# Linear attention and MLP, two layers: loads reordered, key projections split, output buffers shared, new instruction lists

## The chip, the cores and the metric

One core of a Trainium2 chip. The metric is the device time in microseconds of one execution, as the median of several runs. Engines: PE (TensorE, matrix products), DVE (VectorE), ACT (ScalarE), POOL (GpSimd), and SP (SyncE), which here only issues DMA transfers. PE writes into PSUM banks; the others read these.

## The reference

Two identical layers, each an attention block and an MLP block, on x of 2048 rows by 512 columns in bf16:

```python
def _A_ref(x, wqkv, wo):          # H = 32 heads of 16
    q, k, v = qkv[0], qkv[1], qkv[2]
    phi = lambda t: jnp.where(t > 0, t + 1, jnp.exp(t)) + 1e-6
    pq, pk = phi(q), phi(k)
    kv = jnp.einsum("bhsd,bhse->bhde", pk, v)
    z = jnp.einsum("bhsd->bhd", pk)
    num = jnp.einsum("bhqd,bhde->bhqe", pq, kv)
    den = jnp.einsum("bhqd,bhd->bhq", pq, z)[..., None] + 1e-6
...
def _B_ref(x, w1, b1, w2, b2):    # F = 1792
    y = _layernorm(x, axis=-1)
    h = _gelu(jnp.einsum("bsd,df->bsf", y, w1) + b1)
    return jnp.einsum("bsf,fd->bsd", h, w2) + b2
...
x = x + _A_ref(_layernorm(x, axis=-1), A_wqkv, A_wo)
x = x + _B_ref(_layernorm(x, axis=-1), B_w1, B_b1, B_w2, B_b2)
```

The last two lines stand there twice, with the same weights.

## The kernel before

The 2048 rows are 16 tiles of 128 rows, in four chunks of four tiles. In the first attention block the chunks are worked in the order 3, 0, 1, 2, so tiles 12 to 15 come first. All weights stay in SBUF. Names carry the layer, then the tile or chunk: `K0_12` is the key projection of tile 12 in layer 0.

**The steps of an attention block.** A tile of x is normalized (`stats`, `aggr` on DVE, `veps` and `pow` for the reciprocal root, then `cen` and `ysc`, or `norm`). Its normalized rows are transposed, by PE (`PT...`, then a copy `tc...` on ACT) or by a DMA transpose that SP issues (`TA...` before attention, `TB...` before the MLP, `TP...` for queries). `K` multiplies by the key weights: four products of 512 columns, one for each 128 rows of the weights. `Q` does so with the query weights. phi is an exponential and a relu on ACT (`exp`, `relu`), a clipped sum (`min`) and a sum (`phi`) on DVE or POOL; phi(K) goes into one of eight buffers `pk`. `G` accumulates y-transposed times phi(K) over all tiles, so that the value projection is applied once at the end (`KV`), masked to heads (`kvm`) and multiplied by wo (`M`). `Z` and `zs` sum phi(K); `D` gives the denominators, and `WO` the block's output, added to x by `RA`. In layer 1, G is summed by chunk on DVE (`ga`, `gt`) before KV.

**The steps of the MLP.** `W1` (line L1133) is the up-projection: four products for each of 14 blocks of hidden columns. For chunk 0 it is done in halves of two tiles, 256 columns at a time (names end in `_0` and `_1`); for the others on all four tiles, 512 columns. ACT applies gelu. `W2` (L1171) is the down-projection of a tile in two half-sums of seven products (`_0` and `_7`), and `RB` adds it to x. In the last MLP `RB` writes to one of two buffers `outb`, which `OD` stores from SP's queue. The very last tile, 15, is done in two column halves of 256 (`h0`, `h1`; L1158, L1163, L1165), each with its own store.

**What sets the order.** Each engine runs one fixed list of names, written out in `CONF["ORDER"]`. A planner (`Scheduler`) walks the lists with estimated durations and hands out buffers and PSUM banks in the order of that plan; `assign_waits` turns every dependence into a semaphore wait. An engine takes its list strictly in order, so a late operand holds all behind it. DMA issues are entries of the SP, ACT or POOL list.

**The start.** SP's list begins `x0 x1 wk0 x2 wq xc0 xc1 xc2`: the rows of tile 12, of tile 13, the first half of the key weights, the rows of tiles 14 and 15 (`x2`, 256 KB), the query weights (`wq`, 512 KB), then chunks 0, 1 and 2. ACT issues the second half of the key weights (`wk1`). While nothing can be multiplied PE runs dummy products of constants (`warm`: eight of 512 columns and `N_WARM2` of 128; `idle0_0` and `idle0_1`: `N_IDLE` of 128 after each of the first two transposes).

Of the kernel before, what the change touches and what calls it, by code (L numbers as in the profile page):

```python
# [6 lines left out]
BF16 = mybir.dt.bfloat16  # L7
# [20 lines left out]
DMA_LAT = 800.0  # L28

# [81 lines left out]
class Scheduler:  # L111
# [12 lines left out]
    def run(self):  # L124
# [13 lines left out]
        bus = 0.0  # L138
        for _ in g.ops:
            best = None  # L140
            for e in ENGINES:
                if len(self.order[e]) == len(queue[e]):
                    continue
                o = queue[e][len(self.order[e])]
                if o.missing:
                    continue
                at = max(o.ready, free[e])
                if o.table is not None and o.table != table:
                    at = max(o.ready, free[e] + TABLE_LOAD)
# [17 lines left out]
            dur = o.dur  # L167

            if o.fast and pool_busy > at:
                dur += pool_busy - at - 60.0  # L170
            if o.fast:
                dve_busy = at + dur
            if e == "pool" and o.sem is None and o.dur > 300.0:
                dur += max(0.0, min(dve_busy - at, 400.0))
                pool_busy = at + dur
# [92 lines left out]
def assign_waits(graph, order, sems, dma_sems):  # L268
# [10 lines left out]
    while len(done) < total:  # L279
        moved = False  # L280
        for e in ENGINES:
# [43 lines left out]
    N_WARM2=1, N_IDLE=[4, 3], XQ='sp', WKQ='sp act', WK1=1,  # L325
    LAND={'x0': 3210, 'x1': 3930, 'wk1': 5300, 'wk0': 6430, 'x2': 6950, 'wq': 8450, 'xc0': 9730, 'xc1': 11020, 'xc2': 12240},
# [5 lines left out]
            "warm PTA0_12 idle0_0 PTA0_13 idle0_1 K0_12 K0_13 PTA0_14 Q0_3_0 Q0_3_2 PTA0_15 K0_14 K0_15 G0_12_0 "  # L332
            "Q0_3_1 G0_13_0 Q0_3_3 G0_14_0 PTA0_1 K0_0 G0_15_0 K0_1 Z0_3 G0_0_0 K0_3 K0_2 Q0_0_2 G0_1_0 Q0_0_0 "
            "K0_8 K0_4 G0_2_0 G0_3_0 K0_6 Q0_0_3 G0_4_0 K0_7 K0_5 K0_10 K0_11 Z0_0 K0_9 Z0_1 Q0_1_2 Q0_1_0 Q0_1_3 "
            "Q0_0_1 Z0_2 G0_5_0 G0_6_0 D0_0_0 D0_0_3 G0_7_0 Q0_1_1 G0_8_0 D0_0_1 G0_9_0 D0_0_2 G0_10_0 G0_11_0 "
            "G0_11_2 D0_1_0 G0_11_1 Q0_2_0 G0_11_3 KV0_0 D0_1_1 KV0_1 KV0_2 D0_1_2 ZR0 KV0_3 Q0_2_1 M0_0 M0_2 M0_1 "
            "M0_3 Q0_2_2 WO0_0_0 WO0_0_1 WO0_0_2 WO0_0_3 D0_1_3 WO0_1_0 WO0_2_0 WO0_3_0 Q0_2_3 WO0_4_0 WO0_6_0 "
            "WO0_7_0 PTB0_0 WO0_5_0 W10_0_5_0 W10_0_1_0 W10_0_7_0 W10_0_9_0 W10_0_6_0 W10_0_3_0 W10_0_2_0 "
            "W10_0_4_0 W10_0_12_0 W10_0_13_0 W10_0_0_0 W10_0_10_0 W10_0_11_0 W20_0_0 W10_0_8_0 W20_1_0 W20_1_7 "
            "W20_0_7 W10_0_8_1 W10_0_1_1 W10_0_7_1 W10_0_9_1 W10_0_5_1 W10_0_12_1 W10_0_0_1 W10_0_3_1 W10_0_11_1 "  # L340
            "W10_0_13_1 W10_1_3_0 W10_1_4_0 W10_1_13_0 W10_1_11_0 WO0_8_0 W10_1_0_0 WO0_9_0 W10_1_2_0 W10_0_6_1 "
            "W10_0_2_1 W10_0_4_1 W10_1_8_0 W10_1_12_0 W10_1_7_0 W10_1_5_0 W10_1_10_0 WO0_11_0 W10_1_6_0 W10_1_1_0 "
            "WO0_10_0 W10_1_9_0 W20_4_0 W20_7_0 W20_7_7 W20_4_7 W20_5_0 WO0_15_0 K1_0 W20_2_0 W20_5_7 W20_6_0 "
            "W20_6_7 K1_1 W10_2_10_0 W10_2_3_0 W10_2_0_0 W10_0_10_1 WO0_14_0 W10_2_13_0 WO0_12_0 W10_2_6_0 "
            "WO0_13_0 W20_2_7 W10_2_11_0 W10_2_5_0 W10_2_8_0 W10_2_7_0 W10_2_1_0 W10_2_4_0 W10_2_2_0 W10_2_9_0 "
            "W10_2_12_0 W20_9_0 W20_8_0 W20_9_7 W20_8_7 W20_3_0 W20_3_7 W20_10_0 W20_11_0 K1_4 K1_2 W10_3_1_0 "
            "W10_3_7_0 W10_3_8_0 W10_3_5_0 W20_10_7 W10_3_0_0 W10_3_3_0 W20_11_7 W10_3_9_0 W10_3_6_0 W10_3_10_0 "
            "W10_3_2_0 K1_3 W10_3_13_0 W10_3_4_0 W10_3_12_0 W10_3_11_0 K1_8 K1_5 G1_0_1 G1_0_3 G1_0_0 K1_6 G1_0_2 "
            "W20_12_0 K1_7 W20_12_7 W20_13_0 W20_13_7 W20_14_0 K1_9 K1_10 G1_1_0 W20_15_0 W20_15_7 W20_14_7 K1_11 "
            "Q1_1_1 Q1_1_0 G1_1_1 G1_1_3 G1_1_2 Q1_0_0 K1_13 K1_12 Q1_1_2 G1_2_1 Q1_0_2 K1_14 K1_15 Q1_0_1 Q1_1_3 "  # L350
            "ZH1 Q1_0_3 Z1_3 G1_2_2 G1_3_1 D1_0_0 ZR1 G1_2_0 D1_0_2 G1_3_2 D1_0_1 G1_3_3 G1_3_0 G1_2_3 Q1_3_0 "
            "KV1_0 KV1_1 Q1_3_1 KV1_2 D1_0_3 Q1_3_2 KV1_3 Q1_2_0 M1_1 M1_0 M1_3 M1_2 Q1_2_1 WO1_0_0 Q1_3_3 WO1_0_1 "
            "WO1_1_0 WO1_0_2 WO1_0_3 WO1_3_0 WO1_2_0 Q1_2_2 WO1_5_0 WO1_4_0 PTB1_1 Q1_2_3 PTB1_0 WO1_6_0 "
            "W11_0_13_0 W11_0_10_0 W11_0_12_0 W11_0_4_0 WO1_7_0 W11_0_0_0 W11_0_5_0 W11_0_7_0 W11_0_1_0 W11_0_3_0 "
            "W11_0_11_0 W11_0_6_0 W11_0_9_0 W11_0_8_1 W11_0_11_1 W11_0_4_1 W11_0_3_1 W11_0_8_0 W11_0_0_1 W11_0_5_1 "
# [12 lines left out]
            "normA0_3 tcA0_1 expk0_0 expq0_3_3 reluq0_3_3 expk0_1 reluk0_1 normA0_8 normA0_6 reluk0_3 expk0_3 "
            "expk0_2 reluq0_0_2 expq0_0_2 normA0_7 expk0_8 normA0_10 expk0_4 reluq0_0_0 normA0_5 reluk0_6 normA0_9 "
            "expq0_0_3 expk0_6 expk0_7 expq0_0_0 expk0_5 reluk0_5 expk0_10 expk0_11 reluk0_11 expk0_9 reluk0_9 "  # L370
            "reluq0_1_2 expq0_1_2 expq0_1_3 expq0_1_0 expq0_0_1 reluq0_0_1 ln0_0_0 ln0_0_3 rec0_0_0 rec0_0_3 "
            "expq0_1_1 ln0_0_1 rec0_0_1 reluq0_1_1 ln0_0_2 rec0_0_2 ln0_1_0 expq0_2_0 rec0_1_0 ln0_1_1 cpz0 "
            "rec0_1_1 cpm0_0 cpm0_1 cpm0_3 ln0_1_2 rec0_1_2 ln0_1_3 rec0_1_3 expq0_2_2 reluq0_2_1 reluq0_2_2 "
            "reluq0_2_3 expq0_2_1 expq0_2_3 b1c tcB0_0 gelu0_0_5_0 gelu0_0_1_0 gelu0_0_9_0 gelu0_0_6_0 gelu0_0_7_0 "
            "gelu0_0_3_0 gelu0_0_4_0 gelu0_0_12_0 gelu0_0_2_0 gelu0_0_0_0 gelu0_0_11_0 gelu0_0_8_0 gelu0_0_10_0 "
            "gelu0_0_13_0 gelu0_0_8_1 gelu0_0_1_1 gelu0_0_9_1 gelu0_0_7_1 gelu0_0_5_1 gelu0_0_12_1 gelu0_0_0_1 "
            "gelu0_0_13_1 gelu0_0_11_1 gelu0_0_3_1 gelu0_1_13_0 gelu0_1_3_0 gelu0_1_0_0 gelu0_1_11_0 gelu0_1_4_0 "
            "gelu0_0_6_1 gelu0_0_2_1 gelu0_1_2_0 gelu0_1_8_0 gelu0_1_12_0 gelu0_1_5_0 gelu0_1_10_0 gelu0_1_6_0 "
            "gelu0_1_7_0 gelu0_1_1_0 gelu0_1_9_0 gelu0_0_4_1 normA1_1 expk1_0 normB0_9 normB0_11 gelu0_2_3_0 "
            "gelu0_0_10_1 gelu0_2_10_0 gelu0_2_13_0 expk1_1 gelu0_2_6_0 gelu0_2_0_0 reluk1_0 gelu0_2_11_0 "  # L380
# [152 lines left out]
def build_kernel(nc, A_x, A_wqkv, A_wo, B_x, B_w1, B_b1, B_w2, B_b2, out, conf=None, report=False):  # L533
# [5 lines left out]
    with ExitStack() as es:  # L539
# [3 lines left out]
        def mksem(name):  # L543
            return Sem(es.enter_context(nc.semaphore(name)), name)

        NT4, NYB, NPK, NER, NGT, NLR, NSTAT, NOUT = 12, 10, 8, 4, 2, 2, 12, 2
        xsb = SB("xsb", [P, ST, D], FP32)
        t4 = SB("t4", [P, NT4, 4 * D], BF16)
        wqkv = SB("wqkv", [P, DT, 3 * D], BF16)
# [818 lines left out]
```

## Time and profile before

| | us |
|---|---|
| median of 3 runs (328.71, 328.74, 331.37) | 328.74 |
| span of the profiled execution | 326.2 |
| PE busy with matmuls | 320.6 |
| DVE busy | 218.7 |
| ACT busy | 197.5 |
| POOL busy | 131.2 |

The span goes from the first to the last instruction of one profiled execution; the runs' time holds what lies around it. The page is read with one warning: a matmul's record is longer than the time by which it holds up the next one, so a busy PE of 98% says that something was always in its pipeline and not that it ran at its best rate. How far apart matmuls start says more. The granted PE clock was 1.000 over the span.

Busy time by stretch (columns: stretch, its length, busy us and number of instructions of PE, weight loads, DVE, ACT and POOL, granted clock, share of DMA, GB/s):

```profile
0.00:20.00 20.00, 17.82 (x102) 8.15 (x103) 14.42 (x46) 16.06 (x29) 9.93 (x27) 1.00 0.51 171
20.00:60.00 40.00, 40.00 (x250) 19.05 (x248) 34.71 (x90) 35.36 (x65) 23.70 (x38) 1.00 0.46 130
160.00:210.00 50.00, 49.71 (x263) 22.95 (x262) 43.59 (x102) 32.11 (x58) 27.18 (x34) 1.00 0.11 22
275.00:327.00 52.00, 48.65 (x240) 23.21 (x237) 9.39 (x16) 17.44 (x28) 1.53 (x1) 1.00 0.14 38
```

### The profile page before, as it was taken

To read this page: it belongs to the slowest core of one execution; us is meant where nothing else is said; L and a number is where in the kernel's file an instruction comes from. 1 tells how busy PE (TensorE), PEld (TensorE's weight loads), DVE (VectorE), ACT (ScalarE), POOL (GpSimd) and SP (SyncE) were. 2 spreads that over 40 slices of the span, in tenths; PEclk is the share of its full clock that TensorE was granted. 3 is DMA by queue.
4 is the path that set the end of the run, shared out by engine and by line. 5 is a ranking of instruction groups with operands and counts; after the bars stand their busy time and mean duration, and the time that the engine had idled before them with its cause. 6 is when DMAs were issued, how large, how long until landed. Compare 5 with 4: busy or idle time off the path is not lost.

```text
span 326.2 us, 4796 instructions
## 1 busy us (share of the span) xinstructions
PE 320.6 (98%) x1724; PEld 158.2 (48%) x1724; DVE 218.7 (67%) x506; ACT 197.5 (61%) x338; POOL 131.2 (40%) x224
## 2 busy tenths in 40 slices
PE   7999999999999999999999999999999999999996
PEld 3444545656544444444444444458644444444453
DVE  4998689989866662535468899999988663300132
ACT  5998889744753387357963395969923553645200
POOL 3465637673238106134139525645811275100000
PEclk9999999999999999999999999999999999999999
DMA  7424662524012400312110200111153233300011
GB/s 239 163 51 92 173 223 62 181 49 81 21 31 48 97 1 2 74 22 55 27 32 19 47 17 0 28 39 36 32 92 72 48 45 69 81 0 2 32 64 50
DMA packets 47028, 20.39 MB, mean 62 GB/s; under 512 B 41948, under 2 KB 45532, under 8 KB 47004
## 3 DMA queue, kind: packets, MB, share of 16 engines
q1 hardware_dynamic: 45676, 15.09, 20.4%
q0 software_dynamic: 1056, 4.72, 4.5%
q10 hardware_dynamic: 272, 0.26, 0.3%
q8 instruction: 14, 0.23, 0.3%
q14 instruction: 10, 0.08, 0.1%
HBM read 8.00 MB, written 2.10 MB: 31 GB/s over the span
## 4 chain that ended last, share of the span: by engine, by line
PE 91%; DVE 4%; DMA 2%; ACT 1%; SPq 1%; issue 1%; ACTq 0%
PE ps L1133 29%; PE ps L1171 26%; PE ps L1101 9%; PE ps L852 9%; PE ps L870 5%; PE ps L953 4%; PE ps L883 3%; PE ps L985 2%; DMA t<-in_A_x_dram 1%; PE ps L1158 1%; DMA t<-yb 1%; DVE t L839 1%; PE ps L1008 1%; PE ps L1077 1%; PE ps L797 1%
## 5 line engine op out<-in xcount | busy, mean ns | idle before, releaser
L1139 ACT ACTIVATE gT<-ps,b1c 128x512 bf16<-128x512 f32 (+1 forms) x140 | 76.9, 601 | 61.2 <-PE ps L1133 60.8
L1133 PE MATMUL ps<-t,w 128*128 128x512 bf16 (+1 forms) x560 | 102.2, 336 | 0.5 <-DMA t<-yb 0.3
L1171 PE MATMUL ps<-w,gT 128*128 128x512 bf16 x434 | 97.3, 379 | 0.0
L1133 PEld LDWEIGHTS ps<-t,w 128*128 128x128 bf16 x560 | 54.4, 98 | 44.5 <-DMA t<-yb 0.7
L1171 PEld LDWEIGHTS ps<-w,gT 128*128 128x128 bf16 x434 | 42.4, 98 | 50.4 <-ACT gT L1139 0.3
L822 ACT ACTIVATE eb<-ps 128x512 bf16<-128x512 f32 x56 | 32.1, 606 | 21.3 <-PE ps L852 20.3
L749 POOL TENSOR_TENSOR rstd<-veps,neghalf 128x1 f32<-128x1 f32 x64 | 36.7, 581 | 8.2 <-DVE veps L747 5.5
L1181 DVE TENSOR_TENSOR outb<-ps,xsb 128x512 bf16<-128x512 f32 x15 | 10.3, 689 | 40.3 <-PE ps L1171 32.1
L734 DVE BATCH_NORM_STATS2 stats<-xsb 128x6 f32<-128x512 f32 x48 | 32.0, 681 | 0.2
L1101 PE MATMUL ps<-gtb,t 128*128 128x512 bf16 x128 | 31.8, 379 | 0.1
L852 PE MATMUL ps<-wqkv,t 128*128 128x512 bf16 x128 | 31.1, 379 | 0.0
L769 ACT ACTIVATE yb<-xsb,nmr,rstd 128x512 bf16<-128x512 f32 x21 | 16.8, 811 | 12.6 <-POOL nmr L766 12.5
L833 ACT ACTIVATE rb<-ps 128x512 bf16<-128x512 f32 x38 | 22.3, 611 | 1.6 <-PE ps L852 0.9
L739 POOL TENSOR_SCALAR veps<-mv 128x1 f32<-128x1 f32 x32 | 7.3, 227 | 38.4 <-DVE mv L736 36.6
L774 DVE TENSOR_SCALAR yb<-xsb,mv,rstd 128x512 bf16<-128x512 f32 x27 | 15.0, 572 | 9.0 <-POOL rstd L749 8.9
L835 DVE TENSOR_SCALAR eb<-eb 128x512 bf16<-128x512 bf16 x46 | 13.6, 306 | 10.9 <-ACT eb L822 10.8
L1118 POOL TENSOR_TENSOR xsb<-xsb,b2b 128x512 f32<-128x512 f32 x14 | 17.0, 1218 | 8.1 <-DVE yb L774 6.5
L870 PE MATMUL ps<-wqkv,t 128*128 128x512 bf16 x80 | 20.2, 379 | 0.0
L747 POOL TENSOR_SCALAR veps<-mv 128x1 f32<-128x1 f32 x28 | 8.4, 305 | 28.0 <-DVE mv L736 26.9
L1101 PEld LDWEIGHTS ps<-gtb,t 128*128 128x128 bf16 x128 | 12.3, 98 | 14.9 <-ACT gtb L966 0.7
L852 PEld LDWEIGHTS ps<-wqkv,t 128*128 128x128 bf16 x128 | 12.0, 97 | 14.7 <-ACT t L807 0.9
L1065 POOL TENSOR_TENSOR t<-t,rr 128x512 bf16<-128x512 bf16 x7 | 7.7, 1100 | 24.4 <-DVE rr L1061 14.1
(103 smaller groups left out, 398.7 us busy)
## 6 DMA issues: line engine op xcount, KB each, us to landing
w<-in_B_w_dram POOLq DMA_DIRECT2D x4, 896.0 KB, 5.9
out_dram<-outb SPq DMA_DIRECT2D x15, 128.0 KB, 2.1
t<-in_A_x_dram SPq DMA_DIRECT2D x3, 512.0 KB, 7.3
t<-yb SPq DMA_TRANSPOSE x56, 2.5
wqkv<-in_A_wqkv_dram SPq DMA_DIRECT2D x1, 512.0 KB, 5.7
wo<-in_A_wo_dram POOLq DMA_DIRECT2D x1, 512.0 KB, 6.6
wqkv<-in_A_wqkv_dram POOLq DMA_DIRECT2D x1, 512.0 KB, 4.5
t<-t SPq DMA_TRANSPOSE x20, 2.5
```

Source lines behind the costliest of these rows:

```text
L734: G.op("dve", lambda e: e.bn_stats(stats[:, s.slot, :], src()), 620, reads=src_keys, writes=[k + "s"], tiles=[s, *src_tiles], prio=prio, n ...
L749: G.op("pool", lambda e: e.tensor_tensor(rstd[:, s.slot:s.slot + 1], veps[:, s.slot:s.slot + 1], neghalf[:], op=ALU.pow), 570, reads=[k + ...
L769: G.op("act", lambda e: e.activation(yb[:, y.slot, :], src(), ACT.Identity, bias=nmr[:, s.slot:s.slot + 1], scale=rstd[:, s.slot:s.slot + 1]),
L822: G.op("act", lambda e: e.activation(eb[:, et.slot, :], bank(bt), ACT.Exp, scale=factor()), 478, reads=[src_key, *more], writes=[f"e{tag}" ...
L833: G.op("act", lambda e: e.activation(rb[:, rt.slot, :], bank(bt), ACT.Relu, scale=factor()), 478, reads=[src_key, *more], writes=[f"r{tag} ...
L852: ins = e.matmul(bank(b), lhsT=yTa(yT)[:, dt, k * P:(k + 1) * P], rhs=wqkv[:, dt, D:2 * D], start=(dt == 0), stop=(dt == DT - 1))
L870: ins = e.matmul(bank(b), lhsT=yTa(yT)[:, dt, k * P:(k + 1) * P], rhs=wqkv[:, dt, 0:D], start=(dt == 0), stop=(dt == DT - 1))
L1101: ins = e.matmul(bank(wb), lhsT=yTa(pq)[:, kt, k * P:(k + 1) * P], rhs=gtb[:, kt, :], start=(kt == 0), stop=(kt == DT - 1))
L1118: G.op("pool" if on_pool else "dve", lambda e: e.tensor_tensor(xsb[:, st, :], xsb[:, st, :], b2b[:], op=ALU.add), 1120 if on_pool else 600 ...
L1133: ins = e.matmul(bank(b, n), lhsT=w1[:, dt, ft * P:(ft + 1) * P], rhs=yTa(yT)[:, dt, k0 * P:k1 * P], start=(dt == 0), stop=(dt == DT - 1))
L1139: G.op("act", lambda e, ft=ft, b=b, k0=k0, k1=k1, n=n: e.activation(gT[:, g.slot, ft * 512 + k0 * P:ft * 512 + k1 * P], bank(b, n), ACT.Ge ...
L1171: ins = e.matmul(bank(b), lhsT=gT[:, g.slot, ft * 512 + k * P:ft * 512 + (k + 1) * P], rhs=w2[:, ft, :], start=(ft == 0), stop=(ft == FT - 1))
```

## The change

The computation is the same, but for the order of the four products summed in two key projections. The edits:

1. SP's list begins `x0 x1 wk0 wq x2`: the query weights are issued ahead of the rows of tiles 14 and 15.
2. `K0_12` and `K0_13` are each split into two pairs of products; the pair on `wk1` goes first (`K0_12_0`), the pair on `wk0` second (`K0_12`).
3. The dummies: `N_WARM2` 1 to 4, `N_IDLE` [4, 3] to [8, 1].
4. The buffers `outb` are gone; the last block writes to the eight phi(K) buffers. There are 12 buffers of normalized rows for 10.
5. The last tile is split into 384 and 128 columns for 256 and 256.
6. All five lists are written anew, after changes in the planner's durations (which act on its plan alone, and so on the buffers handed out).

```diff
+TAIL = 384
...
-    N_WARM2=1, N_IDLE=[4, 3], XQ='sp', WKQ='sp act', WK1=1,
+    N_WARM2=4, N_IDLE=[8, 1], XQ='sp', WKQ='sp act', WK1=1, K_SPLIT=2, K_HALVES=(1, 0),
...
         "pe":
-            "warm PTA0_12 idle0_0 PTA0_13 idle0_1 K0_12 K0_13 PTA0_14 Q0_3_0 Q0_3_2 PTA0_15 K0_14 K0_15 G0_12_0 "
+            "warm PTA0_12 idle0_0 K0_12_0 K0_12 PTA0_13 idle0_1 Q0_3_0 K0_13_0 K0_13 Q0_3_1 PTA0_14 G0_12_0 PTA0_15 "
+            "K0_14 K0_15 Q0_3_3 Q0_3_2 G0_13_0 K0_0 G0_14_0 PTA0_1 G0_15_0 K0_1 G0_0_0 Z0_3 K0_3 K0_2 Q0_0_2 G0_1_0 "
...
-            "W10_0_4_0 W10_0_12_0 W10_0_13_0 W10_0_0_0 W10_0_10_0 W10_0_11_0 W20_0_0 W10_0_8_0 W20_1_0 W20_1_7 "
-            "W20_0_7 W10_0_8_1 W10_0_1_1 W10_0_7_1 W10_0_9_1 W10_0_5_1 W10_0_12_1 W10_0_0_1 W10_0_3_1 W10_0_11_1 "
-            "W10_0_13_1 W10_1_3_0 W10_1_4_0 W10_1_13_0 W10_1_11_0 WO0_8_0 W10_1_0_0 WO0_9_0 W10_1_2_0 W10_0_6_1 "
+            "W10_0_11_0 W10_0_2_0 W10_0_0_0 W10_0_12_0 W10_0_9_0 W10_0_13_0 W20_0_0 W20_1_0 W10_0_0_1 W10_0_2_1 "
+            "W10_0_12_1 W10_0_5_1 W10_0_11_1 W20_0_7 W10_0_4_1 W20_1_7 W10_0_13_1 W10_0_7_1 W10_0_6_1 W10_0_1_1 "
+            "W10_0_3_1 WO0_8_0 W10_0_8_1 W10_0_9_1 W10_0_10_1 W20_2_0 W20_3_0 W20_3_7 W20_2_7 WO0_11_0 W10_1_5_0 "
...
+            "ZR1 D1_0_0 G1_3_0 G1_2_0 D1_0_1 G1_2_3 G1_3_3 G1_3_2 D1_0_2 Q1_3_1 Q1_3_0 KV1_0 D1_0_3 KV1_1 KV1_2 KV1_3 "
...
+            "WO1_5_0 WO1_3_0 PTB1_1 Q1_2_3 PTB1_0 WO1_4_0 WO1_6_0 W11_0_8_0 W11_0_3_0 WO1_7_0 W11_0_10_0 W11_0_7_0 "
+            "W11_0_0_0 W11_0_4_0 W11_0_5_0 W11_0_12_0 W11_0_9_0 W11_0_13_1 W11_0_12_1 W11_0_2_0 W11_0_5_1 W11_0_1_0 "
...
         "dve":
+            "ones statsA0_12 aggrA0_12 vepsA0_12 cenA0_12 negA0_13 yscA0_12 cenA0_13 yscA0_13 mink0_12 statsA0_14 "
+            "statsA0_15 aggrA0_14 aggrA0_15 cenA0_14 phik0_12 cenA0_15 statsA0_0 vepsA0_14 aggrA0_0 statsA0_3 "
...
         "pool":
-            "powA0_9 nmrA0_5 nmrA0_9 vepsA0_11 powA0_11 phik0_6 w2_0 bdm1 wo phiq0_1_2 wv w1_0 phiq0_1_1 pr0_0_2 "
-            "pr0_1_0 pr0_1_1 w1_1 pr0_1_2 pr0_1_3 vepsB0_1 powB0_1 vepsB0_0 powB0_0 w2_1 pz0_2_1 phiq0_2_3 "
+            "nmrA0_7 vepsA0_11 powA0_11 phik0_6 bdm1 w1_0 w1_1 wv wo w2_1 w2_0 phiq0_1_2 phiq0_1_1 pr0_0_2 pr0_1_0 "
...
         "sp":
-            "x0 x1 wk0 x2 wq xc0 xc1 xc2 TA0_0 TA0_3 TA0_2 TA0_8 TA0_4 TA0_6 b1 TA0_7 TA0_10 TA0_5 TA0_11 TA0_9 b2 "
+            "x0 x1 wk0 wq x2 xc0 xc1 xc2 TA0_0 TA0_3 TA0_2 b1 TA0_8 TA0_4 TA0_10 TA0_5 TA0_6 TA0_7 TA0_11 TA0_9 b2 "
...
-            "OD1 TP1_2_1 TB1_12 TB1_14 OD2 TB1_13 TB1_15 OD4 TB1_11 TB1_9 OD5 TB1_8 TB1_10 OD7 OD14 OD6 OD9 OD12 "
+            "TB1_14 TB1_13 TB1_15 TB1_12 TB1_8 TB1_10 TB1_11 OD2 OD6 OD4 TB1_9 OD15_0 OD5 OD14 OD7 OD12 OD10 OD13 OD8 "
+            "OD9 OD11 OD15_1",
...
-        NT4, NYB, NPK, NER, NGT, NLR, NSTAT, NOUT = 12, 10, 8, 4, 2, 2, 12, 2
+        NT4, NYB, NPK, NER, NGT, NLR, NSTAT = 12, 12, 8, 4, 2, 2, 12
...
+            if L == 0 and c == HC and k < cf["K_SPLIT"]:
+                halves = cf["K_HALVES"]
+                for i, h in enumerate(halves):
+                    def part(e, h=h, i=i):
+                        n = DT // len(halves)
+                        for j in range(n):
+                            ins = e.matmul(bank(b), lhsT=yTa(yT)[:, n * h + j, k * P:(k + 1) * P], rhs=wqkv[:, n * h + j, D:2 * D],
+                                           start=(i == j == 0), stop=(i == len(halves) - 1 and j == n - 1))
+                        return ins
...
-                ot = Tile(OUT, f"out{st}")
+                ot = Tile(PK, f"out{st}")
...
-                    cs = slice(h * D // 2, (h + 1) * D // 2)
+                    cs = slice(0, TAIL) if h == 0 else slice(TAIL, D)
```

## The prediction

> **What bounds the kernel now.** I read the first page for engine shares and the chain, then TensorE's own timeline through the first 12 us, then the chain of waits where TensorE restarts late, and last the two ends: the landing times of the loads and the final stores.
>
> ```profile
> PE 320.6 (98%) x1724; PEld 158.2 (48%) x1724; DVE 218.7 (67%) x506; ACT 197.5 (61%) x338; POOL 131.2 (40%) x224
> ...
> PE 91%; DVE 4%; DMA 2%; ACT 1%; SPq 1%; issue 1%; ACTq 0%
> ```
>
> TensorE is the bound: 98% busy, 91% of the chain. Its matmuls run at one 512-column product per 0.216 us (eight in 1.73 us in the chain), a group of four in 0.865, and the change leaves the number of useful ones alone. So only the places where TensorE stands still can be won. First the start:
>
> ```profile
> 4.57 0.40 PE L797 MATMUL ps<-idp,yb 128*128 128x128 bf16 x4 [0.37 <-DVE yb L715]
> 4.80 0.39 PE L690 MATMUL ps<-const-bfloat16-1.0 128*128 128x128 bf16 x4
> 6.14 0.40 PE L797 MATMUL ps<-idp,yb 128*128 128x128 bf16 x4 [0.94 <-DVE veps L747]
> 6.37 0.33 PE L690 MATMUL ps<-const-bfloat16-1.0 128*128 128x128 bf16 x3
> 6.55 1.89 PE L852 MATMUL ps<-wqkv,t 128*128 128x512 bf16 x8
> ```
>
> The first key projections start at 6.55, behind the second tile's transpose, though the first tile's copy ended at 5.99 and the key weights were there. After 8.4 us I list every place where the next matmul starts over 0.06 us later than the last one's 0.216 us allow: 8.44 (0.17), 11.75 (0.19), 20.29 (0.13), 36.4 (0.14), 78.8 (0.41), 203.3 (0.43), 206.1 (0.19), 210.4 (0.10), 247.05 (0.28), 272.07 (0.42). From 19 us on that is 2.1 us, 2.3 with the small change. The chain shows the large ones:
>
> ```profile
> 78.56 0.25 issue
> 78.81 1.24 PE ps L1133 x5
> ...
> 202.07 1.20 DVE gtb L998 x2
> 203.27 0.05 issue
> 203.32 0.62 PE ps L1008 x8
> ...
> 266.75 1.51 SPq L1183
> 268.31 1.19 SPq L784
> 269.54 2.49 DMA t<-yb
> 272.07 4.49 PE ps L1133 x20
> ```
>
> At 78.8 the first full-width up-projection of chunk 1 waits for a transpose issued at 74.74 that landed at 78.72. At 203.3 KV waits for VectorE's sum of G. At 272.07 it is a transpose held on SP's queue by an output store (L1183, 1.51 us). The ends:
>
> ```profile
> wqkv<-in_A_wqkv_dram SPq DMA_DIRECT2D x1, 512.0 KB, 5.7
> t<-in_A_x_dram SPq DMA_DIRECT2D x1, 256.0 KB, 4.8
> ...
> 323.69 0.43 DVE L1163 TENSOR_TENSOR outb<-ps,xsb 128x256 bf16<-128x256 f32 x1 [0.69 <-PE ps L1158]
> 324.14 0.33 SPq L1165 DMA_DIRECT2D out_dram<-outb  x1
> ```
>
> Query weights: issued 2.69, landed 8.4. Rows of tiles 14 and 15: issued 2.19, landed 7.0. The last store is issued 0.48 after the last matmul ends (323.66) and lands at 325.72.
>
> **The start, part by part.** The loads after wk0 share one stream (wk0 in at 6.24, 256 KB more at 6.95, 512 KB more at 8.42). Swapped, the query weights land at 6.24 + 1.47 = 7.7 and tiles 14/15 at 8.4, 1.4 later; each issue takes 0.42 to 0.47 on SP, so nothing behind them moves. The 3 extra warm dummies (0.056 each) and 4 more in the first idle group lie in TensorE's waits of 0.37 and 0.94; without that cover they cost 0.39, and two fewer in the other group give 0.11 back.
> TensorE anew: first copy in at 5.99, so K12 runs 6.07 to 6.93 (the half on wk1, in by 5.5, goes first; wk0 is in at 6.24, before the third matmul at 6.50). The transpose of tile 13 follows to 7.16, then it waits 0.55 for the query weights: Q0_3_0 7.7 to 8.6, K13 to 9.5, Q0_3_1 to 10.35. VectorE meanwhile gets tile 14 at 8.4: two stats at 0.60, two aggregates, centring 0.27 give 10.25, so the transpose of tile 14 is just in time; phi of tile 12 is next (10.6), G12 10.65 to 11.5, transpose 15 to 11.7, K14 to 12.6, K15 to 13.5 (its copy on ScalarE, by 0.57 a scaled exp or relu and 0.48 a copy, is done at 12.55). Carried on alike, thirteen groups and the transposes are through at 18.9; the row of before has thirteen at 18.89. So 0.5 sooner at the start is paid back as a wait for the query weights: net 0. Bounds: -0.3 if all of it is just in time, +1.3 if VectorE, idle for 6.4 to 7.8 in this walk, hands its late start on in full.
>
> **The middle.** Three old sites lose their cause. At 78.8: four half-products of W2 (6.0 us) and two WO groups now come before chunk 1's first up-projection, which moves some 9 us behind its transposes: -0.41. The second half of chunk 0 is reached 3.0 us sooner instead (74.03 to 71.0). It needs TB0_3, issued at 69.45 now; VectorE's norm of tile 3, 8.3 us after that of tile 0 before, has 13 operations ahead of it for 19, about 6.3 us, so its transpose is issued near 67 and lands (2.5 us) near 69.5: no wait. At 272: OD2 goes behind seven transposes on SP: -0.42. At 203 and 206: two Q groups and D (1.95 us) stand between G and KV for one Q group (0.865); the sums of G that KV needs are split 2 and 2 around it, so I take half of 0.72: -0.36. Together -1.2.
> The weight loads move together on POOL's queue (six issues of 0.72 to 1.23, 5.4 us in all, after phik0_6 at 34.6). Queued behind them is phiq0_1_2, which now ends near 42 for 40.76; its reader, D0_1_2, runs at 50.4. The last weights of attention land, at 512 KB in 1.5 us after the first two of 896 KB, near 47, for uses at 49.5 and 51.9. In exchange the 0.74 and 1.23 issues at 53.7 and 59.7 leave POOL's path to WO. Taken at nothing; if a store of 3.6 MB slows the last SP transposes it would be tenths.
> Output through the eight phi(K) buffers: VectorE's 8.2 us of waits for the two old ones end, but TensorE has no late start after 272, so 0. Two more y buffers: no wait on them is seen, 0.
> New late starts can't be read off a trace of another order. One place shows how tight it is: the second layer's first lower-half projection moves from 13th to 10th (4.8 us after the first, for 6.1) while its transpose, issued 221.13 and landing near 223.7 for a start at 224.25, comes about 1.6 sooner by VectorE's list: slack stays 0.5. With slacks of that size I take new late starts at 0.8, a third of what this order leaves; bounds 0 and 3.0 (all that it leaves, and a third more).
>
> **The tail.** The last product has 128 columns for 256: TensorE's total is equal (14 x (0.163 + 0.056) for 28 x 0.109, the 0.056 from KV's groups of four in 0.22). After its end: adding 128 columns takes 0.28 (0.281, the mean of the 128-column mask products on L1027) for 0.43, but the store before it is now issued 0.03 before that end and holds SP 0.33, so the last is issued 0.35 after, for 0.48: -0.1. Bounds -0.2 and +2.0, below.
> The Trainium skill, "DMA: Bandwidth & Descriptors", Specifications, says that a transfer under 512 B makes the DMA engine read, modify and write; these rows are 256 B for 512 B, and by that rule the store would land later, with no price given there. No row here shows a store of such rows.
>
> Sum: 0 - 1.2 + 0.8 - 0.1 = -0.5. The profiled execution is 326.2 us of span, 2.5 under the median 328.74, which I take to lie outside the span and unchanged: 325.7 of span, **328.2 us**.
>
> **Rivals.** (a) The gaps only move: new late starts eat what the old ones give back, 328.7. For it: ten sites came from one order of the same kind. (b) Slower: tiles 14 and 15, 1.4 us late, starve VectorE, which is 0.9 busy in nearly every slice from 8 to 85 us; its 1.3 us idle is never made up and TensorE stands for it before K14, K15 or G13. Decides if tile 14's transpose starts after 10.7. Then +1.3 - 1.2 + 0.8 - 0.1 = +0.8: 329.5. Against: TensorE has had Q groups to run. (c) All old sites close and no new ones open: -2.3 - 0.1, 326.3. (d) A handover goes wrong: an in-order matmul waits one transpose's whole path (stats, pow, norm, 1.2 issue, 2.5 to land, about 5 us) less the slack of 0.5 to 1: 332.5. Against: places walked above have slack. (e) The short rows: if a store of 256-byte rows is a read and then a write, it takes another round of 2.0 (the landing of a 64 KB store), and the -0.1 is lost: 328.2 + 2.1 = 330.3. This is what the rule of the Trainium skill's DMA page would do here.
>
> **Numbers.** Forecast 0.42 (own range 327.4 to 329.0), (a) 0.20, (b) 0.14, (c) 0.10, (d) 0.09, (e) 0.05. The range 326.4 to 330.9 leaves out (d) and most of (c). Over 1% is 3.3 us, about what a measurement can tell: faster than 325.5 lies beyond (c), 0.02; slower than 332.0 is (d), 0.09; within, 0.89.
>
> **What would show it.** First key projection near 6.1, then a wait of 0.4 to 0.7 for the query weights; four groups through by 10.4; no late starts at the first full-width L1133 group of chunk 1 nor after OD2; the sum of late starts after 19 us at 1 to 2 us; last store issued about 0.35 after the last matmul and landing under 2.0 after it. I am wrong if the thirteenth group ends after 19.5, if one late start is over 1 us, or if TensorE's end is not what moves the span.

## The result and the profile after

The changed kernel takes 327.12 us (median of 10 runs, 326.79 to 328.46). The kernel before, run beside it, takes 328.80 (10 runs, 328.25 to 331.37). The ratio is 0.9935, 95% interval 0.9914 to 0.9956. The forecast was 328.2, in 326.4 to 330.9, with an own range of 327.4 to 329.0 that the result misses by 0.3, and "within 1%" with 0.89. The profiled execution has a span of 325.2 us for 326.2, and its own time is 327.02.

So 0.65% was won, 1.7 us between the medians and 1.0 between the spans of the profiled executions, for a forecast of 0.5. The spread moved too: the runs of the kernel before lie 3.1 us apart, nine of the ten of the changed kernel within 0.8.

The engine totals and the shares of the chain on the page of the changed kernel:

```profile
PE 320.5 (99%) x1729; PEld 158.5 (49%) x1729; DVE 220.2 (68%) x506; ACT 193.5 (60%) x334; POOL 133.1 (41%) x224
...
PE 94%; POOL 2%; DMA 2%; DVE 1%; ACT 0%; SPq 0%; issue 0%
```

TensorE is still the bound, and its share of the chain rose from 91% to 94%. The start, in the timeline of TensorE (start, busy time, line; in brackets the wait before it):

```profile
4.20 0.55 PE L699 MATMUL ps<-const-bfloat16-1.0 128*128 128x128 bf16 x4
5.34 0.40 PE L806 MATMUL ps<-idp,yb 128*128 128x128 bf16 x4 [0.59 <-DVE yb L724]
5.58 0.63 PE L699 MATMUL ps<-const-bfloat16-1.0 128*128 128x128 bf16 x8
6.43 1.04 PE L870 MATMUL ps<-wqkv,t 128*128 128x512 bf16 x4 [0.22 <-ACT t L816]
7.31 0.39 PE L806 MATMUL ps<-idp,yb 128*128 128x128 bf16 x4
7.53 0.22 PE L699 MATMUL ps<-const-bfloat16-1.0 128*128 128x128 bf16 x1
7.80 1.04 PE L891 MATMUL ps<-wqkv,t 128*128 128x512 bf16 x4
```

And in the chain of waits (start, duration, what):

```profile
2.19 5.57 DMA wqkv<-in_A_wqkv_dram
7.75 0.05 issue
7.80 1.04 PE ps L891 x4
8.84 0.94 PE ps L870 x4
9.77 0.86 PE ps L891 x4
10.64 0.22 PE ps L806 x4
10.86 0.86 PE ps L974 x4
```

The first key projection runs at 6.43 for the 6.07 of the walk: tile 12's rows (`x0`) landed at 3.91 here, at 3.19 in the execution of before, and over all traces of this study at 3.2 to 4.2. Then TensorE waits for the query weights, which land at 7.75, as worked out. The transpose of tile 14 starts at 10.47, and the thirteenth group ends at 19.04, for 18.89 before.

From 19 us on, all eight late starts of before are gone and four others have come, listed as the prediction lists them: 28.6 (0.15), 176.9 (0.46), 243.7 (0.19), 246.4 (0.08), together 0.88 for 2.1. The largest in the chain: G of layer 1 waits for a phi(K) that POOL makes (L848) from a relu of ScalarE (L842), which stands behind a norm there (L778):

```profile
174.31 0.81 ACT yb L778
175.12 0.49 ACT rb L842
175.61 0.07 issue
175.69 1.16 POOL pkb L848
176.85 0.05 issue
176.90 1.04 PE ps L1006 x4
```

The tail, in the timeline of all engines:

```profile
321.80 0.78 PE L1180 MATMUL ps<-w,gT 128*128 128x128 bf16 x11
...
322.62 0.29 DVE L1185 TENSOR_TENSOR pkb<-ps,xsb 128x128 bf16<-128x128 f32 x1
322.94 0.45 SPq L1187 DMA_DIRECT2D out_dram<-pkb  x1
```

TensorE ends at 322.58, 1.1 before the 323.66 of before. The last store is issued 0.36 behind it (0.48 before) and lands at 324.68, 1.74 after its issue (1.58 before).

So one profile set beside the other tells a simple story: the lists closed the late starts. The runs below take it apart.

### The profile page after: what moved, and what is told of

It is laid out like the page before. It is cut to its first block, busy times and chain, and to the rows that moved or that the text cites. A ratio compares the mean times of both kernels' runs of the same rounds, so it can differ in the third digit from the quotient of the medians.

```text
span 325.2 us, 4792 instructions
## 1 busy us (share of the span) xinstructions
PE 320.5 (99%) x1729; PEld 158.5 (49%) x1729; DVE 220.2 (68%) x506; ACT 193.5 (60%) x334; POOL 133.1 (41%) x224
## 4 chain that ended last, share of the span: by engine, by line
PE 94%; POOL 2%; DMA 2%; DVE 1%; ACT 0%; SPq 0%; issue 0%
PE ps L1154 30%; PE ps L1193 27%; PE ps L1122 9%; PE ps L861 7%; PE ps L891 5%; PE ps L1006 4%; PE ps L974 4%; PE ps L904 3%; DMA wqkv<-in_A_wqkv_dram 2%; PE ps L1180 1%; PE ps L1098 1%; POOL pkb L848 1%; PE ps L955 1%; PE ps L1029 1%; PE ps L1052 1%; PE ps L806 0%
## 5 line engine op out<-in xcount | busy, mean ns | idle before, releaser
L1193 PE MATMUL ps<-w,gT 128*128 128x512 bf16 x434 | 98.6, 379 | 0.0
L1203 DVE TENSOR_TENSOR pkb<-ps,xsb 128x512 bf16<-128x512 f32 x15 | 10.2, 680 | 34.1 <-PE ps L1193 34.1
L861 PE MATMUL ps<-wqkv,t 128*128 128x512 bf16 x120 | 29.3, 379 | 0.0
L842 ACT ACTIVATE rb<-ps 128x512 bf16<-128x512 f32 x38 | 22.3, 597 | 8.6 <-PE ps L861 6.2
L1199 DVE TENSOR_TENSOR xsb<-ps,xsb 128x512 f32<-128x512 f32 x16 | 10.8, 680 | 19.4 <-PE ps L1193 17.9
L778 ACT ACTIVATE yb<-xsb,nmr,rstd 128x512 bf16<-128x512 f32 x21 | 16.8, 811 | 9.5 <-POOL nmr L775 9.5
L891 PE MATMUL ps<-wqkv,t 128*128 128x512 bf16 x80 | 20.1, 379 | 0.1
L861 PEld LDWEIGHTS ps<-wqkv,t 128*128 128x128 bf16 x120 | 11.3, 98 | 13.9 <-ACT t L816 0.6
L974 PE MATMUL ps<-pkb,yb 128*128 128x512 bf16 x64 | 16.4, 379 | 0.0
```

The lines of the kernel that those rows point to most:

```text
L778: G.op("act", lambda e: e.activation(yb[:, y.slot, :], src(), ACT.Identity, bias=nmr[:, s.slot:s.slot + 1], scale=rstd[:, s.slot:s.slot + 1]),
L842: G.op("act", lambda e: e.activation(rb[:, rt.slot, :], bank(bt), ACT.Relu, scale=factor()), 569 if by else 478, reads=[src_key, *more], w ...
L861: ins = e.matmul(bank(b), lhsT=yTa(yT)[:, dt, k * P:(k + 1) * P], rhs=wqkv[:, dt, D:2 * D], start=(dt == 0), stop=(dt == DT - 1))
L891: ins = e.matmul(bank(b), lhsT=yTa(yT)[:, dt, k * P:(k + 1) * P], rhs=wqkv[:, dt, 0:D], start=(dt == 0), stop=(dt == DT - 1))
L974: ins = e.matmul(ps[:, gb.slot + dc, :], lhsT=yb[:, y.slot, dc * P:(dc + 1) * P], rhs=pkb[:, pk.slot, :], start=(st == FIRST), stop=(st == ...
L1193: ins = e.matmul(bank(b), lhsT=gT[:, g.slot, ft * 512 + k * P:ft * 512 + (k + 1) * P], rhs=w2[:, ft, :], start=(ft == 0), stop=(ft == FT - 1))
```

## The experiments

The first theory was the prediction's own: the new lists carry the gain (2.1 us of late starts for 0.88), and the start, the tail, the buffers and the dummies are worth next to nothing. Its first rival: one of the small parts carries it, the loads, the split, the tail, the dummies or the buffers. Another, on what the dummies do, came up after the first eight runs. The ratios are to the kernel before on the same chip.

| run | median (range), us | ratio to before, 95% |
|---|---|---|
| a_loads_back | 327.44 (327.07 to 328.00) | 0.9963 (0.9948 to 0.9978) |
| a_nosplit | 326.95 (326.28 to 327.22) | 0.9942 (0.9922 to 0.9963) |
| a_tail256 | 326.93 (326.43 to 328.48) | 0.9952 (0.9934 to 0.9969) |
| a_dummies_back | 328.33 (327.84 to 329.84) | 0.9990 (0.9970 to 1.0010) |
| b_early | 336.03 (334.41 to 336.47) | 1.0199 (1.0174 to 1.0223) |
| c_late_back | 330.19 (329.51 to 331.56) | 1.0041 (1.0025 to 1.0057) |
| b_buffers_tail | 329.73 (328.90 to 330.33) | 1.0021 (1.0007 to 1.0035) |
| m_od_w1b | 328.22 (327.47 to 330.17) | 0.9978 (0.9958 to 0.9998) |
| d_old_emitted | 328.25 (327.42 to 329.80) | 0.9987 (0.9964 to 1.0010) |
| d_few_emitted | 328.74 (327.60 to 330.04) | 1.0001 (0.9981 to 1.0022) |
| d_new_on_before | 328.99 (328.32 to 329.47) | 1.0013 (0.9995 to 1.0031) |
| d_simple | 326.93 (326.29 to 327.24) | 0.9952 (0.9932 to 0.9971) |

### One part of the change undone

**The loads.** The changed kernel with tiles 14 and 15 ahead of the query weights again, and the planner's landing times with them:

```diff
-            "x0 x1 wk0 wq x2 xc0 xc1 xc2 TA0_0 ...
+            "x0 x1 wk0 x2 wq xc0 xc1 xc2 TA0_0 ...
```

> The changed kernel with one edit undone: on SP's queue the rows of tiles 14 and 15 go ahead of the query weights again (and the planner's landing table as before); all lists else as changed. Theory T (the gain is in the middle of the lists, the start nets nothing): TensorE's list now asks for the query weights third, so Q0_3_0 waits until 8.4 for 7.8 and TensorE ends 0.4 to 0.7 us later: 327.5 to 327.8 for 327.1. Rival S (the start brings the gain): the whole gain goes, 328.5 or more. Rival O (output buffers and tail bring it): 327.1.

Measured: 327.44, 0.3 above the changed kernel. In its chain the wait for the query weights is longer:

```profile
2.69 5.70 DMA wqkv<-in_A_wqkv_dram
8.39 0.05 issue
8.44 1.04 PE ps L891 x4
```

Q0_3_0 starts at 8.44 for 7.80, and the thirteenth group ends at 19.48 for 19.04. That is just under the 327.5 to 327.8 expected. The exchange is worth 0.4 us by the trace and 0.3 by the medians; the intervals of the two ratios overlap.

**The split.** `K_SPLIT=0`, `K0_12_0` and `K0_13_0` out of the list, nothing else.

> The changed kernel with the two key projections whole again (all four products behind both weight halves). Theory T: in the profile the second half of the weights was in at 6.26, before the first key projection at 6.43, so the split is worth nothing: 327.1, 0.2 either way. Rival S: the first projection starts 0.2 to 0.5 later, 327.4 or more.

Measured: 326.95. In its trace both halves of the key weights are in at 6.34, so the whole K0_12 starts at 6.43, as its first half does in the changed kernel. The transpose behind it starts at 7.29, and Q0_3_0 at 7.88, with the landing of the query weights (7.83). The split is worth nothing.

**The tail.** `TAIL = 256` for 384, so the last tile is cut in halves again.

> The changed kernel with the last tile in halves of 256 columns. Theory T, by the prediction: the last store is issued 0.48 after the last matmul for 0.37 and lands 1.6 after issue for 1.74, so the tail is the same within 0.1: 327.1. Rival O (the tail brings the gain): 327.5 or more. By the rule on rows under 512 B the store of 512 B rows would land sooner by more than 0.2: 326.9 or less.

Measured: 326.93. Its last store, of 64 KB, is issued at 322.82 and lands 1.59 later; that of the changed kernel, 32 KB in rows of 256 B, lands 1.74 after its issue and holds SP 0.45 for 0.33. So short rows cost 0.1 to 0.2 where 128 columns less save as much.

**The dummies.** The changed kernel with `N_WARM2=1, N_IDLE=[4, 3]`.

> The changed kernel with the dummies of before (1 of 128 columns after the eight, groups of 4 and 3). Theory T: they lie in waits, 327.1, less than 0.2 either way, and the granted clock rises at the same time give or take its own scatter. Rival S (the dummies bring the clock up sooner or keep it up): a full clock later by some tenths of a us or lost in the wait before the first key projection, 327.5 or more.

Measured: 328.33, over 1 us worse, and not at the start: the thirteenth group ends at 19.1. Two late starts of 0.54 (103.3) and 1.20 (245.4) appear. The dummies' durations are part of the planner's plan, which hands out buffers, so this run alone could not tell the dummies from another plan. The runs under "Only the dummies" can.

### Old lists and new ones mixed

**The first block.** The kernel before, with the names of the start and of the first attention block set into its lists in the order of the change; dummies and buffers as before.

> The kernel before with the new lists and load order for the first attention block alone (loads, tile norms, K, Q, phi, G, KV, M of layer 0, weight loads on POOL), put into the old lists' places; no split, old dummies, old buffers, old tail, old lists from the first MLP on. Theory T: thirteen groups through at 18.9 as before, 328.6 to 329.0. Rival S: 327.2 to 327.8.

Measured: 336.03. Fragments of two orders do not fit: the late starts of WO between 55 and 64 us come to 4.5 us, and behind the longest of them TensorE runs slowly for a while. Busy time by stretch (columns as in the table of before: stretch, length, five engines, granted clock, DMA share, GB/s):

```profile
58.00:62.00 4.00, 2.89 (x12) 1.01 (x12) 3.93 (x9) 1.00 (x2) 0.74 (x2) 1.00 0.00 0
62.00:64.30 2.30, 0.10 (x2) 0.06 (x2) 0.66 (x2) 2.22 (x5) 2.07 (x3) 1.00 0.21 43
64.30:68.40 4.10, 4.10 (x12) 1.48 (x13) 2.74 (x6) 0.34 (x1) 0.00 (x0) 0.61 0.08 12
```

After 2.3 us without products the granted clock is 0.61 in the next 4.1 us: twelve matmuls started, for some nineteen at one per 0.216. Its start is slow as well: half the clock from 7.16 to 10.57, and the thirteenth group ends at 20.57 for 18.89. All five runs have a mean granted clock of 0.990 or 0.995. The run says nothing on the change's order as a whole, but it shows what a wait can cost beside its own length.

**The end.** The changed kernel, with the old order from the second layer's output projection on: WO, the MLP, the stores and the queries that lie among them.

> The changed kernel with the old order of the second layer's output projection and MLP and of the stores, put into the new lists' places. Theory T: the late starts of before at 210 (0.10), 247 (0.28) and 272 (0.42) come back and those of the changed kernel at 243.7 and 246.4 (0.28) go: +0.5, 327.6. Rivals S and O (the order of this part is worth nothing): 327.1.

Measured: 330.19. The late starts at 209 (0.70), 213 (0.85), 248 (0.70), 273 (0.32) and 307 (0.59) come to 3.2 us. The old order of the end is 3 us worse behind the new order of the middle, though in its own list the late starts from 206 us on come to 1.0: what an order is worth belongs to the whole list.

**Buffers and tail alone.** The kernel before, with output in the phi(K) buffers, 12 y buffers and a tail of 384 and 128.

> The kernel before with outputs in the phi(K) buffers, 12 y buffers and the last tile in 384 and 128 columns; lists, loads and dummies as before. Theory T: VectorE's waits for output buffers end but TensorE does not move: 328.7, 0.2 either way. Rival O: 327.8 or less.

Measured: 329.73, 0.9 worse. The old sites stay, two of them grown (0.62 at 78.9, 0.40 at 247.3); a new late start of 0.95 us comes at 306.5:

```profile
304.21 1.52 PE ps L1167 x7
305.74 0.02 issue
305.76 0.70 DVE pkb L1177
306.46 0.05 issue
306.51 0.60 PE ps L1167 x2
```

A half-sum of W2 waits for VectorE to have read a bank (L1177). The lists are those of before, so what differs is what the planner hands out with other buffers and another tail; which of the two does it was not tried apart. Alone, the two are a loss.

**Two old sites by hand.** The kernel before, with OD2 behind two transposes on SP, and one half-product of W1 with its gelu put ahead of chunk 1:

```diff
-OD2 TB1_13 TB1_15
+TB1_13 TB1_15 OD2
...
-W10_0_13_1 W10_1_3_0 W10_1_4_0 ... W10_0_6_1
+W10_0_13_1 W10_0_6_1 W10_1_3_0 W10_1_4_0 ...
```

> The kernel before with two small moves: the store of tile 2 behind two transposes on SP's queue, and one half-width up-projection of chunk 0 (with its gelu) ahead of the first of chunk 1. Theory T (a closed site is a gain): the late starts at 78.8 and 272.1, 0.41 and 0.42, go, nothing opens behind them, 328.0. Rival M (the gaps only move): another site opens by as much, 328.6 to 328.9.

Measured: 328.22, some 0.7 better than before. The site at 272 is gone, that at 78.8 fell from 0.41 to 0.29, the one at 247 grew to 0.55. By these sites 0.3 should be won; the interval of the ratio holds 0.1 to 1.4, so closing a late start seems to pay, and the size stays rough. Its profiled execution is a long one (329.9, span 328.2), and in it, by shape, from 6.5 to 10.2 us:

```profile
L849 PE MATMUL ps<-wqkv,t 128*128 128x512 bf16 x8 | 3.4, 611 | 0.0
```

The same eight products, K0_12 and K0_13, in the execution of before:

```profile
L852 PE MATMUL ps<-wqkv,t 128*128 128x512 bf16 x8 | 1.9, 378 | 0.0
```

Their starts are 0.427 us apart for 0.216. They take from 6.89 to 10.16, 3.27 us for 8 x 0.216 = 1.73: 1.5 us are lost. No wait shows it. That gave theory **C**: with few dummies in the waits of 4.2 to 6.5 us, some executions have half the clock over the first projections, and the new dummies prevent that. Its rival **N** is the prediction's own step, that the dummies lie in waits and are worth nothing.

### Only the dummies

In the first three of these the plan, the lists, the buffers and the waits stay as they are. Only the number of dummy products that is really issued differs (shown with the numbers of the first run):

```diff
+            real = {"warm": [D] * cf["N_WARM"] + [P] * 1, "idle0_0": [P] * 4, "idle0_1": [P] * 3}[name]
-            return G.op("pe", lambda e: run_idle(e, sizes), sum(sizes) / 1.2, ...
+            return G.op("pe", lambda e: run_idle(e, real), sum(sizes) / 1.2, ...
```

**The old number (1, 4, 3) in the changed kernel.**

> The changed kernel with its plan, orders and buffers untouched; only the number of dummy matmuls that TensorE really runs is the old one (8 + 1 of them at the start, 4 before and 3 after PTA0_13, for 8 + 4, 8 and 1). Theory N (the dummies lie in waits and are worth nothing, as predicted): 326.8 to 327.4 us, 128x512 key matmuls at 379 ns in the profile, no late start that the changed kernel has not. Theory C (fewer dummies let the clock fall to half over the first key projections in some executions, as the eight matmuls of 611 ns in the profile of m_od_w1b read): some of the 10 or more times 1.5 to 3.5 us above the fastest, median up by 0.3 to 1.7 to 327.4 to 328.8, the fastest still about 326.8.

**Fewer still (1, 1, 1).**

> As d_old_emitted, with still fewer dummies really run (8 + 1, 1 and 1), so the waits of 4.2 to 6.4 us are nearly bare. Theory N: 326.8 to 327.4 again. Theory C: the long executions are the more frequent ones, median 328.5 to 330.5, key matmuls of 128x512 near 600 ns in the profile if that execution is one of them.

**The new number (4, 8, 1) in the kernel before.**

> The kernel before with its plan, orders and buffers untouched; only the dummies really run are those of the change (8 + 4, 8 and 1). Theory N: as before, 328.3 to 328.9, the same spread up to 330.9. Theory C: the long executions go (none over 1 us above the fastest of its own), median 327.6 to 328.2, and the fastest no faster than before's fastest, 327.5. If it comes out slower than before by 0.4 or more, the dummies are not wholly in the waits.

Measured: 328.25, 328.74 and 328.99. N is refuted by the first two: with five dummies fewer, and nothing else changed, the changed kernel is back at 0.9987 of the kernel before, and the interval (0.9964 to 1.0010) lies above that of the change (0.9914 to 0.9956). The fastest of its twelve runs (327.42) is slower than the slowest of the nine of d_simple (327.24), measured beside it. C is borne out as far as it goes. With the fewest dummies the twelve times fall into two groups, six from 327.60 to 328.26 and six from 329.23 to 330.04, 1.6 apart in the mean, and the profiled execution is of the upper group (329.54). Its granted clock by stretch:

```profile
6.00:8.00 2.00, 1.37 (x12) 0.81 (x11) 0.62 (x2) 1.50 (x4) 0.47 (x2) 0.95 1.08 387
8.00:10.00 2.00, 2.00 (x7) 0.67 (x5) 1.69 (x5) 1.67 (x4) 0.28 (x1) 0.50 1.04 414
10.00:12.00 2.00, 2.00 (x8) 0.80 (x7) 2.00 (x10) 1.66 (x3) 0.00 (x0) 0.70 0.62 248
```

Half the clock from 7.8 to 11.2 us, and eight products take 3.35 us for 1.73: 1.6 lost (the sixteen key and query products up to 12 us, half of them slow, read 494 and 506 ns in the mean, for 382 and 380). Counted over the runs of the new order, those over 1.2 us above the fastest of their own kernel are 6 of 12 with the fewest dummies, 4 of 24 with the old number (a_dummies_back, d_old_emitted), and 2 of 53 with the new (changed kernel, a_loads_back, a_nosplit, a_tail256, d_simple). By itself 4 of 24 against 2 of 53 says little; 6 of 12 does. In the kernel before, 10 of 31 runs are that long and none of the 12 with the new dummies, and the spread falls from 3.0 us (327.55 to 330.54) to 1.15, close to the 1.0 that C gave.

Two kinds of slow start lie under this. In m_od_w1b every matmul from 0.83 us on starts at the slow distance (0.107 us for 128 columns, 0.427 for 512), and the full rate comes for the first time near 10 us; in the thirteen other traces it comes between 3.5 and 6.1. That execution left no record of its clock, which the views then show as 1.00. In d_few_emitted the clock was up at 4.39 and fell back from 7.80 to 11.21. Three of its six long runs have a mean granted clock of 0.995, which is what 3.41 us at half the clock make in 328 us; the other three and all six short ones have 1.000. No run of the kernel before is under 0.999, so that its long runs are of the first kind is argued from the one trace of m_od_w1b.

What lets the clock fall can be narrowed down. Its changes lie in steps of 3.41 us: up at 4.39, down at 7.80, up at 11.21 in d_few_emitted; up at 3.75, down at 7.16, up at 10.57 in b_early, and down there once more at 65.18, 18 such steps after the first rise, until 68.60. In the 3.41 us ahead of these three falls TensorE was busy for 1.66, 1.64 and 1.21 us. In the 3.41 us behind the first rise of the traces whose clock stayed up it was busy for 1.96 (a_dummies_back) or more: 2.10 in the kernel before, 2.54 in the changed one, and at least 2.2 in every trace with the new dummies and a record of the clock. So in these traces the clock falls when the busy time of such a step is under a bound between 1.66 and 1.96 us, and the new dummies keep clear of it. The Trainium skill ("TensorE: Matmul & The Clock Gate", What's actually happening) has the clock halved after an idle window of about 3.4 us, in a free-running window; the traces agree on the length, 3.41 us, and on the fall coming in some executions only. But the window ahead of it was not idle here: in d_few_emitted TensorE was busy for 1.66 of its 3.41 us.

C is not enough, though. The profiled execution of d_old_emitted is the fastest of its twelve, with a full clock, and still has a span of 325.7 for 325.2, though its start was 0.5 us sooner than that of the changed kernel. And in the kernel before the new dummies raised the median by 0.5 and the fastest run by 0.8, for which C has no reason; nor do the dummies hold the start up there, for the first key projection starts at 6.11 for 6.55. What differs is a late start some 235 us after the last dummy. The chain of d_old_emitted there:

```profile
239.51 0.46 DVE yb L784
239.97 0.28 DVE lr L1075
240.25 4.03 DMA t<-yb
244.29 0.05 issue
244.33 1.69 PE ps L1155 x7
```

The transpose TB1_5, issued at 240.25, takes 4.03 us to land, and the up-projection W11_1_4_0 stands 1.16 for it. From the DMA view of d_old_emitted between 240.2 and 244.4 us (a queue: packets, MB, share; then issues: median us to landing):

```profile
q8 instruction: 1, 0.02, 1.4%
...
t<-yb SPq DMA_TRANSPOSE x1, 4.0
```

The same transpose in the changed kernel, issued at 241.27, between 241.2 and 243.8, where no packet of q8 is seen:

```profile
t<-yb SPq DMA_TRANSPOSE x1, 2.4
```

The packet on q8 is a load of instructions: 16,384 bytes, from 242.27 on, 0.93 us long. A transpose reports its landing in sixteen parts. Fifteen parts of TB1_5 have landed by 242.69, 2.44 after its issue, as in the changed kernel; the sixteenth lands at 244.29, 1.6 later. The two 4-byte packets of it that are still missing run at 243.19, when the load is through. The changed kernel has this load too, but earlier, in the view from 238.5 to 240.7:

```profile
q8 instruction: 1, 0.02, 2.6%
...
t<-yb SPq DMA_TRANSPOSE x2, 3.4
```

There it meets TB1_4 (3.73 to land), and TB1_7 behind it takes 3.16; the matmul has to wait for TB1_5 anyway. That is theory **F**: a load of instructions delays the transpose that it meets by 1.0 to 1.8 us, one of the sixteen parts at TB1_5, all of them at TB1_4, and whether a matmul stands for that hangs on which transpose it meets. Each trace has 13 or 14 such loads on q8. In the changed kernel there is one for every 106 to 139 matmuls and as many weight loads, though the time between two varies from 15 to 28 us; that fits TensorE's own stream, but the trace does not name the engine. So products added or left out at the start shift the later loads against the program. Over all traces with the new order of this stretch:

| trace | matmuls | eleventh load at, us | meets (us to land) | TB1_5, us to land | late start of W11_1_4_0 |
|---|---|---|---|---|---|
| changed kernel | 1729 | 238.6 | TB1_4 (3.73) | 2.40 | 0.19 |
| a_loads_back | 1729 | 238.8 | TB1_4 (3.70) | 2.38 | 0.10 |
| a_nosplit | 1729 | 238.4 | TB1_4 (3.72) | 2.40 | 0.19 |
| a_tail256 | 1729 | 237.6 | TB1_6 (4.02) | 2.38 | 0.30 |
| d_simple | 1729 | 238.0 | TB1_4 (3.46) | 2.39 | under 0.06 |
| a_dummies_back | 1724 | 243.3 | TB1_5 | 4.07 | 1.20 |
| d_old_emitted | 1724 | 242.3 | TB1_5 | 4.03 | 1.16 |
| d_few_emitted | 1719 | 244.4 | TB1_5 | 3.98 | 1.11 |

Eight of eight, in two groups with nothing between. It also explains a_dummies_back: another plan is not needed for its late start of 1.20, since d_old_emitted keeps the plan and has it too. In the kernel before, the new dummies bring the tenth load to 222.2 from 224.7, and there it meets TB1_3: fifteen parts land by 222.68, the sixteenth at 224.47, 4.19 after the issue for 2.41 in the kernel before, and a late start of 1.16 appears at 224.56. The eleventh load, at 241.4, meets TP1_3_3 as it did at 241.2, but lasts 1.63 us for 1.02; the transpose lands after 4.67 for 3.94, SP's issue of the next is held 2.77 for 2.06, and the late start at 247 to 248, behind a later transpose of that queue, grows from 0.28 to 0.94. So the same edit takes one load off the path in one order and puts another on it in the other.

F holds beyond this stretch. The fourteen traces have 910 transposes that are issued after 50 us. The 747 during which no load of instructions runs all land 2.39 to 2.56 us after their issue. The other 163, which meet one (16,384 bytes on q8 or 8,192 on q14), take 2.40 to 4.67, and every transpose over 2.56 is among them. Even old late starts that were put down to the order come from this. At 78.8 the kernel before waits for TB0_4; its DMA view between 74.7 and 78.8:

```profile
q8 instruction: 1, 0.02, 1.6%
...
t<-yb SPq DMA_TRANSPOSE x1, 4.0
```

Fifteen parts have landed by 77.21, the sixteenth at 78.72; the load runs from 76.62 to 77.67. With the new dummies and the same order that load runs at 73.57, TB0_4 lands after 2.49, and the late start at 78.8 is gone. At 272 a load at 266.49 meets TB1_14 (3.89 to land) and the store OD2 behind it, which holds SP for 1.51 us where a store that meets no load holds it for 0.33 to 0.58. With the 0.28 at 247 these are 1.1 of the 2.1 us of old late starts.

The Trainium skill ("Runtime: NRT & Kernel Launch", Instruction fetch mechanics) says that instructions are refilled in blocks of 16 KiB, 256 of them, and that crossing a boundary is mostly hidden. The size agrees. No wait of TensorE for its instructions is seen here; what is not hidden is what the load does to the transposes.

**Without the two idle edits.** The changed kernel without the split and with `TAIL = 256`.

> The changed kernel without the split of the two key projections and with the last store cut in two equal parts (TAIL 256), the two edits that were worth nothing alone. Sum of the two runs: 0.2 + 0.2 below the changed kernel at most, 326.6 to 327.1; if they pay in the same place, 326.9. Over 327.4 would say that a wait fills the place of one of them.

Measured: 326.93, as each edit alone. Neither edit is needed; the version is simpler and no faster than the changed kernel within what is measured.

## Why the prediction came out as it did

**The start: net 0.** Right, and by the steps given. First key projection at 6.43 for 6.1, then a wait for the query weights (0.3 to the landing at 7.75, for 0.55), thirteenth group 19.04 for 18.9. That 0.5 sooner is paid back as that wait is read from the trace: a_nosplit shows only that the split adds nothing, and a_loads_back that without the exchange Q0_3_0 starts 0.6 later and the thirteenth group ends 0.4 later.

**The middle: -1.2, and new late starts +0.8.** The second term was right in the profile (0.88). The first was too small: not only the sites at 78.8, 203, 206 and 272 closed, and those in full, but all eight, 2.1 us. The four sites named could be argued from list and trace, the other four (0.65 together) could not. And of the four, those at 78.8 and 272 had another cause than the order: each lay behind a transpose that met a load of instructions. The prediction read 3.98 us to land at the one and an issue of 1.51 at the other, and did not ask what made them so long. The new order closed both, but d_new_on_before closes the first with the old order as well. Yet all of this holds for the order together with its dummies: with the old number of them issued, the changed kernel loses its lead in the median.

**The dummies: "lie in TensorE's waits".** This is the step that failed. That they cost nothing where they stand is right. That they do nothing else is wrong: d_old_emitted is 1.1 us above the changed kernel in the median and 0.6 in the fastest run (327.42 for 326.79), and 1.3 above d_simple on the same chip. Two mechanisms: the load of instructions that meets TB1_5 (1.16 for 0.19 of late start, 1.0 us) and the half clock in some executions (some 1.6 us each). The forecast of -0.5 had no term for either. How the median divides between the two was not measured apart; as an estimate, without its two long runs the median of d_old_emitted is 328.21 for 328.25, so the clock has little part in it, and without its six long runs that of d_few_emitted is 328.0 for 328.74.

**The tail: -0.1.** Issue 0.36 after TensorE's end for 0.35 forecast; landing 1.74 for 1.58, which the sum took as unchanged. Together +0.04 for -0.1, and a_tail256 says 0 within the measurement.

**The buffers: 0.** Nothing in the changed kernel speaks against it, but it does not hold alone: with the old lists, buffers and tail together lose 0.9 (b_buffers_tail).

**Span and time: 2.5 outside the span.** This size was wrong too. In the 93 runs of the kernel before that were measured beside the experiments the time is 1.69 to 1.89 above the span of the same execution, in the profiled one of the changed kernel 1.82. So the profiled execution of before, of 326.2 us, was one of about 328.0, 0.7 under the median of 328.74; with 1.8 for 2.5 the forecast would have been 327.5. The profiles show 1.0 us won, and the other 0.7 lies in how much longer the kernel before runs in most executions than in the one that was profiled.

**The rivals.** (a) Gaps only move: no, they fell by more than half. (b) The late tiles starve VectorE: no; the point of decision was 10.7 for tile 14's transpose, and it ran at 10.47. (c) All old sites close and none opens, 326.3: the old ones did close, and 0.88 opened; 327.12 lies nearer to this rival, which had 0.10, than to the forecast. (d) A handover goes wrong by 5 us: not in the change; b_early shows it for a mixture of orders. (e) Short rows: a penalty of 0.15, not another 2.0; the rule of the Trainium skill ("DMA: Bandwidth & Descriptors", Specifications) is seen at most in that.

## What to carry to other kernels

An edit of the number of instructions shifts every later load of instructions: before a late start behind a DMA is put down to an order, look whether such a load lies in that transfer, and compare a trace with a few instructions more. Where a wait at the start can't be closed, fill it with dummy work and judge that by the spread of many runs, since one profile may show either clock. An order written out by hand is worth something only as a whole; pieces of two good orders gave the slowest kernel of the study.

## What the runs showed of the hardware

A load of 16,384 bytes of instructions takes 0.88 to 1.63 us. A transpose that meets none lands 2.39 to 2.56 us after its issue (747 of 747 after 50 us); one that meets a load takes up to 4.4 us (4.7 in d_new_on_before), often with fifteen of its sixteen parts on time. A load that ends within half a microsecond of the issue costs it nothing (TA1_13 in the changed kernel, 2.43). TensorE's clock falls to half for 3.41 us after 3.41 us in which it was busy for 1.66 or less, and stays up after 1.96 or more, as far as these traces show. Whether a load moved to another place in the stream (by a dummy elsewhere, say) would free TB1_5 with the old dummies too was not tried.
